# Two-layer attention and gated-MLP kernel: the first two head groups of layer two take turns by key pairs, and head outputs are turned by DMA

## The chip, the cores and the metric

The kernel runs on one core of a Trainium2 chip. Five engines work side by side: PE (TensorE, matmuls into PSUM), ACT (ScalarE), DVE (VectorE), POOL (GpSimd) and SP (SyncE, here only a queue that issues DMA). The metric is the device time of one execution in microseconds.

## The reference

Two layers of multi-query attention, each followed by a gated MLP with a mixing matrix over the sequence. S = 2048 rows, D = 512, 32 heads of 16 with one shared key and value head, F = 1792.

```python
def _A_ref(x, wq, wk, wv, wo):
    q = (x @ wq).reshape(B, S, 32, 16).transpose(0, 2, 1, 3)
    k, v = x @ wk, x @ wv
    p = softmax(einsum('bhqd,bkd->bhqk', q, k) * 16 ** -0.5)
    return einsum('bhqk,bkd->bhqd', p, v).transpose(0, 2, 1, 3).reshape(B, S, 512) @ wo

def _B_ref(x, w_in, w_sp, b_sp, w_out):
    z = gelu(x @ w_in)
    z1, z2 = z[..., :896], layernorm(z[..., 896:])
    g = einsum('ts,bsf->btf', w_sp, z2) + b_sp[None, :, None]
    return (z1 * g) @ w_out

x = x + A(layernorm(x)); x = x + B(layernorm(x))     # layer one
x = x + A(layernorm(x)); x = x + B(layernorm(x))     # layer two, same weights
```

## The kernel before

**Order of the work.** Every operation is handed to a planner (class `Sched`) with an estimated duration, its dependences and a priority. The planner plays the whole kernel through on paper and fixes one instruction order for each engine; on the chip each engine takes its instructions in that order and waits on semaphores. So a small edit can move instructions all over the program.

**Attention.** The rows are cut into query chunks of 512, 512, 512, 256, 128 and 128 (`chunks`). A head group is 4 heads of 512 query columns (or more heads of fewer columns); there are 32 groups a layer, in pairs that share one query set: `kT` holds the keys twice, masked for the even and for the odd half of the heads (`v` = 0 and 1). A unit is one key tile of 128 rows in one group, with four blocks (one for each head row group of 32), each a score matrix of 128 keys by 512 queries. A key pair is two key tiles, and units are worked off in pairs.

Scores (`_qk`, L1710) go into a ring of PSUM banks: `self.ring = [(0, 3), (3, 2)]`, that is banks 0 to 2 and banks 3 and 4 in turn. `FillStream` fills one half, `ExpStream` (L1382) takes the exp of the other half on ACT in one instruction of 3 or 2 blocks (128x1536 or 128x1024) into the SBUF ring `Pa`. While ACT works on one half, PE fills the other. Some blocks go to DVE instead (`DexStream`: L1566, then a chain of five operations L1591 to L1597 on two blocks at a time, into `Pd`), through one of the side banks 5 and 7. `PVStream` (L1458) multiplies the exps with V and accumulates a whole group in bank 6 (`pvb`), four heads side by side. `WarmStream` (L1691) puts in matmuls on zeros where PE would have too little to do.

**End of a group** (`finish_group`): DVE copies bank 6 to `oT` (L826), PE transposes it in four 128x128 pieces into a side bank (L833), DVE takes the reciprocal of the denominators, which come from a column of ones in V (L838), and multiplies (L850) into `on`. When a chunk has all its heads, `project` turns `on` by DMA (L552, for the last two chunks by PE, L886), multiplies by `wo` (L915) and adds to the residual `X` (L919).

**Gated MLP.** `mixer_chunk` normalises, multiplies by `w_in` (L947, L983) and takes the gelu on ACT (L1014, L1018, with table loads). `spatial` multiplies by the mixing matrix in passes over the row tiles that are ready (L1124; its bias starts the first pass with a matmul of 4 rows, L1121), evicted by DVE into `gp` (L1137, L1138). These matmuls run between the attention of the later chunks. The matrix w_sp is transposed by DMA at the start (L591) and kept in a scratch in HBM (L593).

**Closing and the next layer's keys.** The last row tile's part of the mixing can only run when the last chunk is done. `closing` does it in eight steps of 256 rows: matmuls on `z2n` (L1183), a cast to `E` on DVE or ACT (L1194, L1195), add (L1198), multiply with z1 (L1201), matmul with `w_out` (L1216), add to the residual (L1221). After each step, in layer one, `layer_keys` builds one key pair of layer two: layernorm (`ln`: L637 to L652, transposed by DMA, L552, or by PE, L669), keys (L699) and values (L707) and their copies to `kT` (L719 on DVE, L721 on ACT) and `V`. For the value matmul the weight stands four times side by side, padded to 128 columns (`wv_rep`), so that the result has the four copies that P.V reads. During the closing the score ring has only what the key pairs so far allow: group 0 of layer two over the key tiles that exist. `gate` holds DVE's exps of layer two back until the closing has read its buffers.

The units are worked in the order of their list, group after group:

```python
for k in range(self.NT):
    u = Unit()
    u.grp, u.kt, u.index, u.pv = g, k, len(self.units), None
```

Of the kernel before, what the change touches and what calls it, by code (L numbers as in the profile page):

```python
# [13 lines left out]
P = 128  # L14
# [359 lines left out]
LOOK = 7  # L374
# [35 lines left out]
class Group:  # L410

    __slots__ = ("layer", "ci", "v", "t0", "n", "units", "q", "evac", "index")
# [14 lines left out]
class Kern:  # L427
    def __init__(self, nc, A_x, A_wq, A_wk, A_wv, A_wo, B_x, B_w_in, B_w_sp, B_b_sp, B_w_out, out):
# [13 lines left out]
        self.ring = [(0, 3), (3, 2)]  # L442
# [18 lines left out]
        self.wv_rep = sb([P, KD, 128], BF16, "wv_rep")  # L461
        self.wo_r = sb([P, 4, D], BF16, "wo_r")
        self.w_in_r = sb([P, KD, FF], BF16, "w_in_r")
        self.b4 = sb([4, 512], BF16, "b4")
# [22 lines left out]
        self.oT = sb([P, 2, 512], BF16, "oT")  # L487
        self.on = sb([P, 4, D], BF16, "on")
# [42 lines left out]
        sc.lend(1, range(self.ring[1][0], sum(self.ring[1])), None)  # L531
# [26 lines left out]
    def load(self, A_x, A_wq, A_wk, A_wv, A_wo, B_b_sp):  # L558
# [3 lines left out]
        wv_nat = self.z1s[:, 64:128].rearrange("p (kd n) -> p kd n", kd=KD)  # L562
# [7 lines left out]
        lv = self.dma(lambda e: e.dma_start(wv_nat, A_wv.rearrange("(kd p) r -> p kd r", p=P)), (), "ldv", 131072, 1.1,  # L570
# [13 lines left out]
        self.l_b = self.dma(lambda e: e.dma_start(self.b4[:], B_b_sp.rearrange("(k t) -> k t", k=4)), (), "ldb", 4096)  # L584
# [31 lines left out]
        for j in range(4):  # L616
# [5 lines left out]
        m = vm(self.wv_rep[:], 512, 0.12)  # L622
        self.c_wv = rows(self.wv_rep[:].rearrange("p kd (g r) -> p kd g r", r=32)[:, :, :, 0:DH],
                         wv_nat[:, :, None, :].to_broadcast([P, KD, 4, DH]), m, lv, 256, 1.1)
        self.c_wq = [lq[0]] + [lq[1]] * 3
        m = vm(self.V[:], 2048, 0.13)
        self.z1s_free = [self.c_wk, self.c_wv]
# [55 lines left out]
    def layer_keys(self, layer):  # L683
        sc = self.sc
        for p in range(8):
            def build(p=p):
                ts = (2 * p, 2 * p + 1)
                pr = 0.3 if p < 2 else 1.0
                dd = list(self.xnTA_read[p])
                evs = []  # L690
                for tt in ([ts[:1], ts[1:]] if p < 2 else [ts]):
                    evs += self.ln(tt, lambda t: [self.x_op[t]], self.xnTA[:, tt[0]:tt[-1] + 1, :, :], dd, pr, p < 2,
                                   layer == 0)
                self.xnTA_read[p] = []

                def kpe(e, b):
                    ins = None
                    for kd in range(KD):
                        ins = e.matmul(self.b32(b)[:, 0:256], self.wk_rep[:, kd, :], self.xnTA[:, 2 * p:2 * p + 2, kd, :],  # L699
                                       start=(kd == 0), stop=(kd == KD - 1))  # L700
                    return ins

                def vpe(e, b):
                    ins = None
                    for i, t in enumerate(ts):
                        for kd in range(KD):
                            ins = e.matmul(self.b32(b)[:, 256 + 128 * i:384 + 128 * i],  # L707
                                           self.xnTA[:, t, kd, :], self.wv_rep[:, kd, :],
                                           start=(kd == 0), stop=(kd == KD - 1))
                    return ins  # L710

                def kcp(b, v):
                    return self.kT[:, v, p * 256:(p + 1) * 256], self.b32(b)[:, 0:256]

                def vcp(b):
                    return (self.V[:, ts[0]:ts[0] + 2, :].rearrange("p t (c r) -> p t c r", r=32)[:, :, :, 0:DH],
                            self.b32(b)[:, 256:512].rearrange("p (t c r) -> p t c r", t=2, c=4)[:, :, :, 0:DH])
                kd_, vd_ = self.kv_war.get((layer, p), ([], []))
                ks = [dict(fn=lambda e, b, v=v: e.tensor_scalar(*kcp(b, v), self.mask[:, v:v + 1], None, op0=ALU.mult),  # L719
                           dur=d_psum(256), prio=pr - 0.1 + 0.2 * v, deps=kd_ + [self.c_mask[v]],  # L720
                           alts=[("act", lambda e, b, v=v: e.activation(*kcp(b, v), ACTF.Copy, scale=self.mask[:, v:v + 1]),  # L721
                                  d_act(256) + 0.1)]) for v in range(2)]
                vc = dict(fn=lambda e, b: e.tensor_copy(*vcp(b)), dur=d_psum(128), prio=pr, deps=[self.c_v] + vd_,
                          alts=[("act", lambda e, b: e.activation(*vcp(b), ACTF.Copy), d_act(128) + 0.1)])
                if p < 2:
                    _, k = sc.job([(kpe, 4 * d_mm(256))], ks, evs + [self.c_wk], pr)
                    _, (v,) = sc.job([(vpe, 8 * d_mm(128))], [vc], evs + [self.c_wv], 0.9)
                else:
                    _, (k0, v, k1) = sc.job([((lambda e, b: (kpe(e, b), vpe(e, b))[1]), 4 * d_mm(256) + 8 * d_mm(128))],
                                            [ks[0], vc, ks[1]], evs + [self.c_wk, self.c_wv], pr)  # L730
                    k = [k0, k1]
                self.xnTA_ev[(layer, p)] = evs
                for t in ts:
                    self.k_op[(layer, 0, t)], self.k_op[(layer, 1, t)] = k
                    self.v_op[(layer, t)] = v
            if layer == 0:
                build()
            else:
                self.key_builders[p] = build
# [5 lines left out]
    def layer_groups(self, layer):  # L745
        t0 = 0
        for ci, n in enumerate(self.chunks):
            ns = 512 // n
            for s0, v in [(s, v) for s in range(0, 4, ns) for v in range(2)]:
                g = Group()  # L750
                g.layer, g.ci, g.v, g.t0, g.n = layer, ci, v, t0, n
                g.index = len(self.groups)
                if v == 0:
                    q = QSet()
                    q.grp, q.s0, q.ns, q.op, q.left, q.reads = g, s0, ns, None, 8 * self.NT, []
                    q.index = len(self.qsets)
                    q.slot = q.index % NQS
                    self.qsets.append(q)
# [16 lines left out]
            t0 += n  # L775

# [44 lines left out]
    def finish_group(self, g, pv_last):  # L821
# [4 lines left out]
        ev = sc.op("dve", lambda e: e.tensor_copy(self.oT[:, par, :], self.b32(self.pvb)), d_psum(512),  # L826
# [9 lines left out]

        def rc(e, b):
            return e.reciprocal(self.rden[:, par, :, :], self.b16(b)[:, 0:512].rearrange(  # L838
                "p (i j r) -> p i j r", i=4, j=4)[:, :, :, DH])

        def nm(h, e, b):
# [4 lines left out]
            else:  # L846
# [4 lines left out]
                out, self.b16(b)[:, s0 * 128:s1 * 128].rearrange("p (i j r) -> p i j r", j=4, r=32)[:, :, :, 0:DH],  # L851
                self.rden[:, par, s0:s1, :, None].to_broadcast([P, s1 - s0, 4, DH]), ALU.mult)
        hs = range(2 if g.n == 256 else 1)
        pl, ops = sc.job([(pe, 0.3)], [
# [212 lines left out]
    def spatial(self, s0, s1, layer):  # L1067
# [28 lines left out]
        for tc in range(4):  # L1096
# [16 lines left out]
            for f in range(NF):  # L1113
                seq = ([] if acc else [None]) + list(range(s0, s1))

                def pe(e, b, part, tc=tc, f=f, w_=w_, seq=seq):
                    ins = None
                    for s in part:
                        st, sp = (s == seq[0]), (s == seq[-1])
                        if s is None:  # L1120
                            ins = e.matmul(self.b32(b), self.ident[0:4, tc:tc + 1].to_broadcast([4, P]), self.b4[:, :],  # L1121
# [129 lines left out]
class FillStream:  # L1251
# [5 lines left out]
    def __init__(self, k):  # L1257
        self.k = k
        self.u = 0
        self.n = 0  # L1260
        self.exp_of = [None, None]
        self.pending = [False, False]
        self.last = []
# [14 lines left out]
    def peek(self, f):  # L1278
# [4 lines left out]
        self.blocks = self.nxt(k.ring[r][1])  # L1283
        if not self.blocks:
            return None
        deps = [self.exp_of[r]]
        for b in self.blocks:
# [8 lines left out]
        if not k.sc.reclaim(r):  # L1296
            return None
        self.deps = [d for d in deps + k.sc.lent_rel(r) if d is not None]
        return (max([d.vis for d in self.deps], default=0.0), 0.0)

    def commit(self, t):
        k = self.k
        r = self.n % 2
        b0 = k.ring[r][0]
# [32 lines left out]
        self.n += 1  # L1337
        self.last = [o]
        k.exp_s.queue.append((r, blocks, o))


class ExpStream:
# [5 lines left out]
    def __init__(self, k):  # L1348
        self.k = k
        self.queue = []  # L1350
        self.slot = 0
        self.owner = [None] * NPA
# [5 lines left out]
    def peek(self, f):  # L1358
        if not self.queue:
            return None  # L1360
        r, blocks, fo = self.queue[0]
        base = (self.k.ring[r][0] + 5 * self.slot) % NPA
# [11 lines left out]
    def commit(self, t):  # L1374
        k = self.k
        r, blocks, fo = self.queue.pop(0)
        base = self.base
        n = len(blocks)
        b0 = k.ring[r][0]
# [10 lines left out]
        if r == 1:  # L1390
            self.slot = (self.slot + 1) % 3
# [3 lines left out]
        if not nx or nx[0].unit.grp.layer != blocks[0].unit.grp.layer:  # L1395
            k.sc.lend(r, range(b0, b0 + k.ring[r][1]), o)
            if not self.queue:
                k.sc.op("act", lambda e: e.activation(k.tiny[:], k.mhalf[:], ACTF.Gelu_apprx_tanh), 0.1, [o, k.c_mh], -2.0,
                        table="gelu")


class PVStream:
# [5 lines left out]
    def __init__(self, k):  # L1408
        self.k = k
        self.u = 0  # L1410
        self.evac = None

    def peek(self, f):
# [16 lines left out]
        if u.first:  # L1430
            if self.evac is not None:
                if self.evac.start is None:
                    return None
                deps.append(self.evac)
            if not k.sc.reclaim("pv"):
                return None
            deps += k.sc.lent_rel("pv")
# [12 lines left out]
    def commit(self, t):  # L1450
# [3 lines left out]
        def fn(e):  # L1454
            ins = None
            for b in u.blocks:
                j = b.j
                ins = e.matmul(k.b32(k.pvb)[32 * j:32 * j + 32, :], k.V[:, u.kt, 32 * j:32 * j + 32], b.slot,  # L1458
# [7 lines left out]
        if u.last:  # L1466
            k.finish_group(u.grp, o)
            self.evac = u.grp.evac
            if self.u == len(k.units) or k.units[self.u].grp.layer != u.grp.layer:
                self.evac.at_commit = lambda ev: k.sc.lend("pv", [k.pvb], ev)  # L1470
# [179 lines left out]
class WarmStream:  # L1650
# [10 lines left out]
    def peek(self, f):  # L1661
# [9 lines left out]
        if u >= len(k.units) or k.units[u].first:  # L1671
# [3 lines left out]
            else:  # L1675
                ev = k.pv_s.evac
                if ev is None or ev.start is None or u >= len(k.units) or k.units[u].grp.layer != k.units[u - 1].grp.layer:
# [8 lines left out]
    def commit(self, t):  # L1686
        k = self.k
        b = self.bank

        def fn(e):  # L1690
            return e.matmul(k.b32(k.pvb if b is None else b.idx), k.zero[:], k.zero[:, None, :].to_broadcast([P, 4, P]),  # L1691
# [71 lines left out]
```

## Time and profile before

| | us |
|---|---|
| median of 8 runs (lowest 1833.04, highest 1837.45) | 1835.0 |
| the profiled execution | 1834.5 |
| its span, first to last instruction | 1832.4 |
| ACT busy in the span | 1739.7 |
| DVE busy | 1697.8 |
| PE busy | 1599.4 |

PE's busy time holds 327.3 us of matmuls on zeros. The mean granted TensorE clock is 0.993 of full speed. Exps of three blocks show 1600 ns each and exps of two 1176 ns; since one starts before the other has wholly ended, these durations overlap, and the union of all 1430 exps is 1625.2 us. In the lists below, a row names the source line, the engine, the operation, what it writes and reads, and in brackets the idle time before it with what ended it.

### The profile page before, as it was taken

What the parts mean: (1) busy time and instruction counts of PE and PEld (TensorE: products, weight loads), DVE (VectorE), ACT (ScalarE), POOL (GpSimd) and SP (SyncE); (2) the same over time, 40 slices, a digit from 0 to 9 for tenths busy, and PEclk for the clock granted to TensorE, in tenths of its full rate; (3) what the DMA queues carried; (4) which work ended last, traced back from release to release, by engine and by line L of the source; (5) the groups of instructions that cost most, each with busy time, mean ns of one, the idle gap of its engine ahead of it and who ended that gap; (6) DMA issues with size and microseconds to landing.
All of it is one profiled execution on the core that took longest, in us unless ns stands there. A gap on an engine that the chain in (4) does not pass through costs nothing.

```text
span 1832.4 us, 30222 instructions
## 1 busy us (share of the span) xinstructions
PE 1599.4 (87%) x11863; PEld 480.3 (26%) x11947; DVE 1697.8 (93%) x2924; ACT 1739.7 (95%) x1565; POOL 49.1 (3%) x89
## 2 busy tenths in 40 slices
PE   8888888888899998998888888888888999999988
PEld 3222222222222222223432222222222222222234
DVE  8999999999989899887889999999999998998868
ACT  8999999999999999999579999999999999999983
POOL 1000000000000000000100000000000000000000
PEclk9999999989999999999999999999999999999999
DMA  9800010001000111202210000100010000201123
GB/s 264 214 1 1 12 35 1 1 1 21 16 28 24 47 24 36 64 27 56 65 37 1 1 1 13 35 1 1 1 21 12 33 24 24 47 27 41 58 57 111
DMA packets 122964, 68.04 MB, mean 37 GB/s; under 512 B 76996, under 2 KB 119240, under 8 KB 122824
## 3 DMA queue, kind: packets, MB, share of 16 engines
q1 hardware_dynamic: 121240, 65.95, 13.4%
q8 instruction: 95, 1.56, 0.4%
q14 instruction: 45, 0.37, 0.1%
q10 hardware_dynamic: 1584, 0.16, 0.1%
HBM read 30.97 MB, written 17.83 MB: 27 GB/s over the span
## 4 chain that ended last, share of the span: by engine, by line
ACT 42%; PE 22%; DVE 18%; issue 17%; POOL 1%; DMA 0%; ACTq 0%; POOLq 0%
ACT Pa L1382 40%; PE ps_all L1710 6%; PE ps_all L1124 6%; PE ps_all L1458 4%; DVE E L1566 3%; DVE Pd L1597 3%; PE ps_all L1216 2%; PE ps_all L1691 1%; DVE E L1593 1%; DVE E L1591 1%; DVE E L1595 1%; DVE st L637 1%; PE ps_all L915 1%; DVE E L1594 1%; DVE gp L1137 1%
## 5 line engine op out<-in xcount | busy, mean ns | idle before, releaser
L1382 ACT ACTIVATE Pa<-ps_all 128x1536 bf16<-128x1536 f32 (+1 forms) x1430 | 1625.2, 1388 | 14.3 <-PE ps_all L1710 12.4
L1710 PE MATMUL ps_all<-qs,kT 32*128 32x512 bf16 x4096 | 562.7, 386 | 179.7 <-ACT Pa L1382 163.8
L1566 DVE TENSOR_SCALAR E<-ps_all 128x512 f32<-128x512 f32 x522 | 356.0, 685 | 26.1 <-PE ps_all L1710 22.4
L1691 PE MATMUL ps_all<-zero 128*128 128x512 bf16 x1051 | 327.3, 391 | 17.4 <-ACT z1s L1014 3.2
L1710 PEld LDWEIGHTS ps_all<-qs,kT 32*128 32x128 bf16 x4096 | 138.7, 91 | 734.7 <-ACT Pa L1382 685.6
L1458 PE MATMUL ps_all<-Pa,V 128*32 128x512 bf16 x3574 | 324.2, 387 | 0.2 <-ACT Pa L1382 0.2
L1597 DVE SCALAR_TENSOR_TENSOR Pd<-E 128x1024 uint16<-128x1024 f32 (+1 forms) x262 | 318.2, 1214 | 4.1
L1124 PE MATMUL ps_all<-wsT,z2n 128*128 128x512 bf16 x655 | 187.4, 382 | 7.5 <-issue 4.1
L1593 DVE TENSOR_TENSOR E<-E 128x1024 f16<-128x1024 f16 (+1 forms) x262 | 179.2, 684 | 5.2
L1458 PE MATMUL ps_all<-Pd,V 128*32 128x512 bf16 x522 | 183.3, 386 | 0.0
L1595 DVE TENSOR_TENSOR E<-E 128x1024 f16<-128x1024 f16 (+1 forms) x262 | 178.7, 682 | 3.7
L1591 DVE TENSOR_SCALAR E<-E 128x1024 f16<-128x1024 uint16 (+1 forms) x262 | 179.0, 683 | 1.3
L1691 PEld LDWEIGHTS ps_all<-zero 128*128 128x128 bf16 x1051 | 79.8, 98 | 186.5 <-issue 126.8
L1594 DVE TENSOR_SCALAR E<-E 128x1024 f16<-128x1024 f16 (+1 forms) x262 | 109.3, 417 | 1.8
L1137 DVE TENSOR_TENSOR gp<-ps_all,gp 128x512 f16<-128x512 f32 x112 | 75.4, 685 | 26.2 <-PE ps_all L1124 25.9
L1458 PEld LDWEIGHTS ps_all<-Pa,V 128*32 128x32 bf16 x3574 | 64.7, 94 | 121.3 <-issue 117.0
L1124 PEld LDWEIGHTS ps_all<-wsT,z2n 128*128 128x128 bf16 x714 | 54.0, 97 | 98.9 <-issue 59.1
L947 PE MATMUL ps_all<-w_in_r,xnTB 128*128 128x448 bf16 x256 | 63.1, 356 | 1.3 <-DVE E L1566 1.0
L983 PE MATMUL ps_all<-xnTB,w_in_r 128*128 128x512 bf16 (+2 forms) x336 | 61.8, 310 | 0.5 <-DVE z1s L994 0.4
L1216 PE MATMUL ps_all<-E 128*128 128x512 bf16 x215 | 51.6, 380 | 4.7 <-DVE E L1201 3.0
L1195 ACT ACTIVATE E<-ps_all 128x512 f16<-128x512 f32 (+1 forms) x52 | 24.6, 550 | 24.0 <-PE ps_all L1183 24.0
L826 DVE CAST oT<-ps_all 128x512 bf16<-128x512 f32 x64 | 43.8, 685 | 2.9 <-PE ps_all L1458 2.6
(87 smaller groups left out, 949.7 us busy)
## 6 DMA issues: line engine op xcount, KB each, us to landing
wsT_scratch<-gp SPq DMA_DIRECT2D x16, 512.0 KB, 3.8
wsT<-wsT_scratch SPq DMA_DIRECT2D x8, 1024.0 KB, 5.4
z1s<-z_scratch SPq DMA_DIRECT2D x16, 448.0 KB, 3.8
wsT<-wsT_scratch SPq DMA_DIRECT2D x8, 512.0 KB, 3.8
z_scratch<-z1s SPq DMA_DIRECT2D x4, 896.0 KB, 6.4
X<-in_A_x_dram SPq DMA_DIRECT2D x8, 256.0 KB, 5.6
out_dram<-X SPq DMA_DIRECT2D x16, 128.0 KB, 1.9
w_in_r<-in_B_w_in_dram SPq DMA_DIRECT2D x1, 1792.0 KB, 10.0
```

Source lines behind the costliest of these rows:

```text
L1124: ins = e.matmul(self.b32(b), self.z2n[:, s, f * 128:(f + 1) * 128], w_[:, s - s0, :] if s - s0 < na or not spare else wsp[:, s - s0 - na, :],
L1137: return e.tensor_tensor(dst, self.b32(b), dst, ALU.add)
L1382: return e.activation(k.Pa[:, base:base + n, :], k.b32(b0, n).rearrange("p (k q) -> p k q", k=n), ACTF.Exp, scale=SCALE)
L1458: ins = e.matmul(k.b32(k.pvb)[32 * j:32 * j + 32, :], k.V[:, u.kt, 32 * j:32 * j + 32], b.slot, tile_position=(0, 32 * j), start=u.first, ...
L1566: c = k.sc.op("dve", lambda e: e.tensor_scalar(k.ey[:, s, 512 * i:512 * (i + 1)], k.b32(j.bank.idx)[:, 0:512], E_LOG2, E_BIAS, op0=ALU.mul ...
L1591: o2 = sc.op("dve", lambda e: e.tensor_scalar(x, lo, E_X * 2.0 ** -16, E_X * E_A, op0=ALU.mult, op1=ALU.add), d_sb(n, 0.521e-3), self.ops ...
L1593: o3 = sc.op("dve", lambda e: e.tensor_tensor(w, x, x, ALU.mult), d_sb(n, 0.521e-3), [o2, self.wfree], pr)
L1594: o4 = sc.op("dve", lambda e: e.tensor_scalar(w, w, E_C, None, op0=ALU.add), d_sb(n, 0.26e-3), [o3], pr)
L1595: o5 = sc.op("dve", lambda e: e.tensor_tensor(w, w, x, ALU.mult), d_sb(n, 0.521e-3), [o4], pr)
L1597: o7 = sc.op("dve", lambda e: e.scalar_tensor_tensor(po.bitcast(U16), y, E_D, w, op0=ALU.add, op1=ALU.add), d_sb(n, 1.042e-3), [o5] + self ...
L1691: return e.matmul(k.b32(k.pvb if b is None else b.idx), k.zero[:], k.zero[:, None, :].to_broadcast([P, 4, P]), start=b is not None, stop=b ...
L1710: return e.matmul(self.b32(bank), self.kT[32 * j:32 * j + 32, g.v, kt * 128:(kt + 1) * 128], self.qs[32 * j:32 * j + 32, g.q.slot, :], til ...
```

## The change

- Layer two's first two groups (the two halves of one query set) are interleaved in the list of units: two key tiles of the first, the same two of the second, and so on. The second accumulates in bank 0 (`pvb2`).
- The ring has three shapes. While the last key tile of layer two is not yet placed ("ramp"), banks 1 to 3 alone, one fill of three blocks after another, and bank 4 goes to the side jobs. Then, until the second group's copy is placed ("pair"), banks 1, 2 and banks 3, 4 in turn. Otherwise ("full") as before. A change of shape waits until both exps in flight are done.
- Places in `Pa` are handed out one after another, not by fixed slots.
- `wv_r` has the 16 value columns once; the copy from PSUM writes them four times.
- Except in the last chunk, a group's output is turned by a DMA transpose on SP's queue into `oTt`, and the reciprocal and the product read that; the PE transposes and their side bank are not used.
- The bias rows are padded with zeros to 128 rows, the last key pair of layer two is transposed by PE, and DVE's exps look 6 units ahead, not 7 (`LOOK`).

```diff
-LOOK = 7
+LOOK = 6
...
-        self.ring = [(0, 3), (3, 2)]
+        self.rings = {"full": [(0, 3), (3, 2)], "ramp": [(1, 3), (1, 3)], "pair": [(1, 2), (3, 2)]}
+        self.pvb2 = 0
...
-                                   layer == 0)
+                                   layer == 0 or p >= 7)
...
-                            ins = e.matmul(self.b32(b)[:, 256 + 128 * i:384 + 128 * i],
-                                           self.xnTA[:, t, kd, :], self.wv_rep[:, kd, :],
+                            ins = e.matmul(self.b32(b)[:, 256 + DH * i:256 + DH * (i + 1)],
+                                           self.xnTA[:, t, kd, :], self.wv_r[:, kd, :],
...
+        if layer == 1:
+            ga, gb = [g for g in self.groups if g.layer == 1][:2]
+            gb.pvb = self.pvb2
+            self.twin = gb
+            i0 = ga.units[0].index
+            self.units[i0:i0 + 2 * self.NT] = [u for i in range(0, self.NT, 2) for g in (ga, gb) for u in g.units[i:i + 2]]
+            for i, u in enumerate(self.units[i0:i0 + 2 * self.NT]):
+                u.index = i0 + i
...
+        if g.ci < len(self.chunks) - 1:
+            tr = self.transpose(self.oTt[:, par, :].rearrange("p (i r) -> p i r", i=4), self.oT[:, par, :],
+                                [ev, self.rd_read[par]], f"oq{par}", 0.5)
+            self.oT_read[par] = tr
+            m = sc.op("dve", lambda e: rc(e, None), 0.18, [tr], 0.6)
+            for h in hs:
+                m = sc.op("dve", lambda e, h=h: nm(h, e, None), d_psum(256 // len(hs)), [m] + onr, 0.5)
+                self.norms.append(m)
...
+        mode = "full"
+        if self.blocks[0].unit.grp.layer == 1:
+            o = k.k_op.get((1, 0, k.NT - 1))
+            if o is None or o.start is None:
+                mode = "ramp"
+            elif k.twin.evac is None or k.twin.evac.start is None:
+                mode = "pair"
+            else:
+                deps.append(k.twin.evac)
+        if mode != self.mode:
+            if any(self.pending):
+                return None
+            deps += self.exp_of
...
-        self.n += 1
+        self.n += 2 if self.mode == "ramp" else 1
...
-        base = (self.k.ring[r][0] + 5 * self.slot) % NPA
+        base = self.pos if self.pos + len(blocks) <= NPA else 0
```

## The prediction

> **What bounds the kernel now.** I read the page first (busy shares), then the stretches, then ACT's waits, then the timeline of the one stage in which ACT has holes.
>
> ```profile
> span 1832.4 us, 30222 instructions
> PE 1599.4 (87%) x11863; PEld 480.3 (26%) x11947; DVE 1697.8 (93%) x2924; ACT 1739.7 (95%) x1565; POOL 49.1 (3%) x89
> ...
> ACT  8999999999999999999579999999999999999983
> ```
>
> ACT is the bound: 1739.7 of 1832.4 us, so 92.7 us idle in all. Its row of tenths has two holes, in the middle (5, 7) and at the end (8, 3). The stretches size them (columns: PE, PEld, DVE, ACT, POOL busy, TensorE clock, DMA).
>
> ```profile
> 860.00:880.00 20.00, 18.69 (x115) 7.80 (x115) 13.54 (x25) 8.94 (x11) 0.55 (x1) 1.00 0.00 1
> 880.00:900.00 20.00, 16.03 (x118) 9.20 (x118) 18.68 (x55) 10.57 (x23) 2.81 (x5) 1.00 0.24 66
> 900.00:920.00 20.00, 17.72 (x126) 7.68 (x127) 19.02 (x53) 14.36 (x20) 3.05 (x6) 1.00 0.35 89
> 920.00:940.00 20.00, 16.73 (x110) 6.62 (x111) 14.29 (x37) 12.16 (x16) 1.52 (x4) 1.00 0.26 50
> 940.00:960.00 20.00, 16.85 (x126) 5.84 (x124) 17.01 (x33) 15.76 (x17) 1.29 (x3) 0.91 0.13 27
> 980.00:1000.00 20.00, 16.77 (x129) 4.29 (x129) 19.56 (x32) 20.00 (x19) 0.00 (x0) 1.00 0.00 1
> ```
>
> From 860 to 960, where layer one closes and layer two's keys appear, ACT is idle 38.2 us, while DVE is at 18.7 and 19.0 of 20 until 920. The last row is steady attention: ACT full, DVE 98%. Within the hole, ACT's own timeline from the first exp of layer two:
>
> ```profile
> 903.65 6.88 ACT L1382 ACTIVATE Pa<-ps_all 128x1024 bf16<-128x1024 f32 x6 [0.44 <-PE ps_all L1710]
> 915.03 0.47 ACT L721 ACTIVATE kT<-ps_all,mask 128x256 bf16<-128x256 f32 x1 [4.50 <-PE ps_all L707]
> ...
> 935.05 0.60 ACT L1195 ACTIVATE E<-ps_all 128x512 f16<-128x512 f32 x1 [3.56 <-PE ps_all L1183]
> 936.13 1.51 ACT L1195 ACTIVATE E<-ps_all 128x512 f16<-128x512 f32 x3 [0.48 <-PE ps_all L1183]
> 942.55 0.47 ACT L721 ACTIVATE kT<-ps_all,mask 128x256 bf16<-128x256 f32 x1 [4.91 <-PE ps_all L707]
> ```
>
> The waits of 4.50 and 4.91 us end at a key: group 0 has used up every key pair. That is what the change aims at. From 943.74 on ACT is nearly full again. After 903.65 the holes sum to 16.4 us; the 20.8 us before it lie in the tail of the layer, with no score to work on, and the change gives nothing there.
>
> **The change part by part.** Counts come from the instruction orders of the two programs as built, times from the one profiled execution, 1834.5 us (1832.4 of span and 2.1 around it); the median of the runs is 0.5 higher.
>
> *Price of a score block.* Between 79.08 and 240.99 ACT did 143 exps without a gap: 161.9/71.5 = 2.264 us for a pair of 3 and 2 blocks, 0.453 a block. Refills start 0.91 us apart across an exp of 2 blocks and 1.35 across one of 3, so exps of 2 alone cost 0.455 a block.
>
> 1. *Exps.* 714 to 707 of 3 blocks, 716 to 724 of 2; P.V matmuls that read DVE's exp go from 522 to 528. Six blocks fewer on ACT: 6 x 0.453 = -2.7 us. DVE gets three more chains (2 x 0.685 + 0.685 + 0.686 + 0.418 + 0.684 + 1.219 = 5.06 us each, 15.2 in all); its 134.6 us of idle time cover that, at 760 to 860 above all (13 to 17 of 20). If not, P.V of those units is late next, then the exp that wants its buffer.
>
> 2. *Other ACT work.* Layer one loses four key copies of 0.42 net and the V-weight copy of 0.42, and gains a 1024-wide copy (about 1.0), a query copy and a V copy; four 512-wide casts in the closings go to DVE. I take -0.6 us.
>
> 3. *Ramp: two groups on the same keys.* Until the last key tile is planned, scores use one buffer of three banks (1 to 3), with no double buffering. An exp of 3 is 1.60 us to its end, the fill starts 0.07 later, and exp follows fill by 0.43 (903.22 to 903.65): 2.1 us for 3 blocks against 1.35. PE stands in order behind each fill that waits, and the closing's matmuls behind it. I walked the order from the first fill: fourteen fills at 2.1, and where PE puts 9 or 10 matmuls of 0.215 between fills, or ACT casts and key copies, about 2.3: near 31 us to the last closing matmul. DVE was busy about 32.3 of the 38.8 us between 903.2 and the last residual add (942.0); four more casts of 0.6, two of 256 fewer at 0.35, and V copies add 2 us. So 31 from PE and ACT, 34 from DVE; with dependences I take 35.3, that is -3.5 us (ends: -5, and +4 if the two delays add up). At that point 42 blocks have been filled where before had 40: -0.9. Then four single-buffered fills follow where before ran full: 4 x 0.75, less 1.2 for query and key copies that fit the gaps: +1.8. Two changes of ring (ramp to pair, pair to full) each empty it once, fill and latency, 0.6: +1.2. Sum -1.4 us. The pair stage itself is 34 exps of 2: 68 x 0.002 = 0.1, nothing.
>
> 4. *Head outputs turned by DMA.* 240 PE transposes go (256 to 16), 60 DMA transposes come on SP's queue. The nearest row, the same shape:
>
> ```profile
> L552 SPq DMA_TRANSPOSE onT<-on x28: 1191/1267/2222, 222.2 to 1667.5; - x28
> ...
> DMA to landing us min/median/max: 2.4/2.5/4.4
> ```
>
> About 2.5 us after the eviction. In the new order DVE has mostly 3.8 us of work between eviction and reciprocal (about 3.3 with overlaps): hidden. Behind that reciprocal stand DVE's exp chains; at 4.4 us a landing costs 1.1 us of DVE. Ends: 0, and 60 x 1.1 = 66 us of DVE, of which little reaches ACT. I take 0, near the median. On SP six of them stand between the w_sp transposes, so SP waits there for each group; the last w_sp store moves from 78 us to about 47.8 + 5 x 25 = 173, still before its first reader at 261 us. Reciprocal and normalisation now read SBUF. The Trainium skill (VectorE: DVE Perf Modes, Why PSUM operands drop a tier) lets one hope for the two-element mode; 16-bit SBUF products of 256 take 0.285 us here, the PSUM form 0.415, so the rule's best is 64 x 0.13 = 8.3 us of DVE. The second operand stays fp32, so I take 0.415 and no gain. PE relief matters only where PE is at 18.5 of 20 (500 to 660, 1420 to 1560, 1640 to 1680), where ACT is idle 6.8 us: -1.5.
>
> 5. *V unreplicated, bias from 128 rows, last key pair turned on PE, LOOK 6.* 128 V matmuls shrink from 128 to 16 columns; PE does not bound, 0. The V copy keeps its 0.28 us. The bias load waits for a POOL memset, covered by 800 us. LOOK acts through the counts above.
>
> 6. *Ends.* The first fill now stands behind the third key pair: about 1 us later, 0.5 got back by fewer copies: +0.5. After the last P.V, layer one has 39 spatial matmuls left against 31, layer two 45 against 40; at 0.215, partly under the head chain: +0.7 and +0.5. Sum +1.7.
>
> Total: -2.7 - 0.6 - 1.4 - 1.5 + 1.7 = -4.5, so 1830.0 on the profiled run, 1830.5 as a median.
>
> **A rule against the change.** PE loses work and waits more. [...]the clock falls already:
>
> ```profile
> 380.00:400.00 20.00, 16.46 (x117) 4.05 (x116) 17.09 (x27) 18.53 (x18) 0.00 (x0) 0.84 0.00 1
> 400.00:420.00 20.00, 17.47 (x130) 4.17 (x129) 19.12 (x29) 19.19 (x18) 0.00 (x0) 0.90 0.00 1
> ```
>
> ACT lost 2.3 us there. The Trainium skill (TensorE: Matmul & The Clock Gate, HAM oscillation) says a gap of over 3.4 us brings half clock; from these clocks, 10.4 us at half rate, priced by the page at half, 5.2 us of PE. The row decides: 2.3. Sixty more dummy matmuls (1051 to 1111) replace what goes, so I count 0 and keep 2.3 for one more episode, 5.2 at the rule's price.
>
> **The rivals.**
> - *The single buffer stretches the closing (slower).* If PE's wait at each fill is not hidden under DVE, 14 waits of 0.75 add 10.5 us to DVE's chain: 34 + 10.5 = 44.5 against 38.8, +5.7 where I have -3.5. Total +4.7: 1839.7. For it: PE is in order and DVE has no slack at 900 to 920. Against: DVE idles at 920 to 940. It decides from 43 us between first fill and last residual add. Chance 0.23.
> - *Two groups fill the hole.* The ramp holes of 16.4 us all but vanish as the closing runs at 31 us and DVE keeps pace: some 6 us beyond my sum, 1824.5. Against: single buffering. Chance 0.21.
> - *It does not do what it says.* 42 blocks against 40 at the closing's end is hardly more exps; then only items 1 and 6 act: 1834. Chance 0.14.
>
> **How the numbers follow.** My case has 0.42, at 1826 to 1835, about six tenths of it beyond the 0.2% (3.7 us) that a measurement of this kernel can tell. Faster (below 1831.3): 0.25 + 0.21 = 0.46. Within: 0.15 of my case, 0.13 of the last rival, 0.02 of the first: 0.30. Slower (above 1838.7): 0.21 of the first, 0.02 of my case, 0.01 of the last: 0.24. Range 1821 to 1841: from the faster rival less a late clock episode to the slower one plus a little.
>
> **What would show it.** First fill to last residual add: 35 us right, 43 the slower rival, 31 the faster. ACT idle from 860 to 960 (38.2) should fall to about 35. DVE waits at the reciprocal on the DMA beyond 10 us in sum would refute item 4, more than 93 us of ACT idle in all the whole forecast.

## The result, and the profile after

| | before | after |
|---|---|---|
| median, us (32 and 11 runs on one chip) | 1834.19 | 1823.35 |
| lowest and highest | 1831.89 to 1840.25 | 1819.3 to 1833.64 |
| ratio, 95% interval | | 0.9939 [0.9928, 0.9949] |
| the profiled execution; its span | 1834.5; 1832.4 | 1824.4; 1822.6 |

The kernel became faster by 10.8 us, or 0.6%. The sum had said 4.5. First the page of the kernel after: span, busy times, and ACT's row of tenths.

```profile
span 1822.6 us, 29937 instructions
PE 1587.7 (87%) x11690; PEld 467.4 (26%) x11775; DVE 1709.5 (94%) x2947; ACT 1735.8 (95%) x1563; POOL 50.8 (3%) x90
...
ACT  7999999999999999999589999999999999999983
```

ACT is still the bound. The 9.8 us by which the span shrank are 3.9 us less work on ACT (1739.7 to 1735.8) and 5.9 us less idle time (92.7 to 86.8). The middle hole, tenths 5 and 7 before, is 5 and 8. The same stretches as before (columns: PE, PEld, DVE, ACT, POOL busy, TensorE clock, DMA):

```profile
860.00:880.00 20.00, 17.69 (x123) 8.41 (x123) 16.30 (x31) 9.13 (x13) 1.10 (x2) 1.00 0.00 1
880.00:900.00 20.00, 16.47 (x116) 9.26 (x119) 19.58 (x59) 10.39 (x24) 2.26 (x4) 1.00 0.30 82
900.00:920.00 20.00, 18.06 (x126) 7.29 (x125) 19.61 (x53) 15.50 (x19) 2.82 (x6) 1.00 0.41 96
920.00:940.00 20.00, 16.84 (x136) 7.50 (x134) 17.00 (x46) 14.74 (x18) 2.98 (x6) 0.91 0.21 41
940.00:960.00 20.00, 16.77 (x140) 4.99 (x140) 19.73 (x33) 19.19 (x22) 0.00 (x0) 1.00 0.00 1
980.00:1000.00 20.00, 16.80 (x131) 4.17 (x131) 19.69 (x32) 20.00 (x19) 0.00 (x0) 1.00 0.00 1
```

The two rows before 900 have hardly moved: there is still no score to work on. From 900 to 960 ACT is busy 49.43 us where it was 42.28. All of ACT's idle time, by stretch:

| stretch, us | idle before | idle after | change |
|---|---|---|---|
| 0 to 20 (first scores) | 8.3 | 9.8 | +1.5 |
| 20 to 840 (layer one) | 5.9 | 2.7 | -3.2 |
| 840 to 860 | 0.0 | 1.9 | +1.9 |
| 860 to 960 (closing, ramp) | 38.2 | 31.05 | -7.2 |
| 960 to 980 (change of ring) | 0.0 | 0.5 | +0.5 |
| 980 to 1700 | 5.4 | 5.2 | -0.2 |
| 1700 to the end | 34.85 | 35.5 | +0.7 |

So the ramp is where most came from. Layer one, which the interleave does not touch, gave 3.2 us up to 840 and took 1.9 of them back. ACT's timeline through the ramp, from the first exp of layer two on:

```profile
901.35 1.45 ACT L1428 ACTIVATE Pa<-ps_all 128x1536 bf16<-128x1536 f32 x1 [1.10 <-PE ps_all L1761]
903.72 1.45 ACT L1428 ACTIVATE Pa<-ps_all 128x1536 bf16<-128x1536 f32 x1 [0.92 <-PE ps_all L1761]
...
935.96 1.45 ACT L1428 ACTIVATE Pa<-ps_all 128x1536 bf16<-128x1536 f32 x1 [1.35 <-PE ps_all L1761]
...
942.35 1.45 ACT L1428 ACTIVATE Pa<-ps_all 128x1536 bf16<-128x1536 f32 x1 [0.50 <-PE ps_all L1761]
943.70 0.47 ACT L722 ACTIVATE kT<-ps_all,mask 128x256 bf16<-128x256 f32 x1
944.28 2.85 ACT L1428 ACTIVATE Pa<-ps_all 128x1024 bf16<-128x1024 f32 x3
947.32 28.61 ACT L1428 ACTIVATE Pa<-ps_all 128x1024 bf16<-128x1024 f32 x31 [0.18 <-PE ps_all L1761]
976.42 60.31 ACT L1428 ACTIVATE Pa<-ps_all 128x1536 bf16<-128x1536 f32 x53 [0.49 <-PE ps_all L1761]
```

Eighteen exps of three blocks (54 blocks) come 2 to 3.7 us apart, each after a wait for the single buffer's refill or beside other ACT work. The pair stage follows at 944.28, and the full ring at 976.42. Of ACT's waits for a key, one of 0.8 us is left. In the list of ACT's waits over the whole run (total, times, longest) the second pair is of before, the first of after:

```profile
ACT Pa L1428 <- PE ps_all L1761: 17.4, 26, 1.7
...
ACT kT L722 <- PE ps_all L708: 0.8, 1, 0.8
```

```profile
ACT Pa L1382 <- PE ps_all L1710: 12.4, 34, 1.0
ACT kT L721 <- PE ps_all L707: 11.1, 6, 4.9
```

The wait for keys fell by 10.3 us, and the wait for refilled scores rose by 5.0, about half as much. In the 120 us after the first exp of layer two, whose rows stand further down, it rose from 2.6 to 9.1: that is the price of the single buffer.

The head outputs (the product of 256 columns and the reciprocal, before and then after; behind them the DMA transposes on the tile `oTt` and their landing):

```profile
L850 DVE TENSOR_TENSOR on<-ps_all,rden 128x256 bf16<-128x256 bf16 x56 | 23.2, 415 | 0.1
L838 DVE RECIPROCAL rden<-ps_all 128x16 f32<-128x16 bf16 x64 | 16.1, 252 | 7.2 <-PE ps_all L833 6.9
```

```profile
L863 DVE TENSOR_TENSOR on<-oTt,rden 128x256 bf16<-128x256 bf16 x52 | 21.6, 415 | 0.1
L851 DVE RECIPROCAL rden<-oTt 128x16 f32<-128x16 bf16 x60 | 14.9, 248 | 3.2 <-DMA oTt<-oT 3.2
```

```profile
L555 SPq DMA_TRANSPOSE oTt<-oT x60: 1189/1192/1541, 49.2 to 1709.0; - x60
...
DMA to landing us min/median/max: 2.4/2.4/4.5
```

DVE stood still for a landing 3.2 us in all, where it had stood 7.2 us for PE's transposes, and the reciprocal takes 248 ns from SBUF where it took 252 from PSUM.

### The profile page after: what moved, and what is told of

It is laid out like the page before. It is cut to its first block, busy times and chain, and to the rows that moved or that the text cites. A ratio compares the mean times of both kernels' runs of the same rounds, so it can differ in the third digit from the quotient of the medians.

```text
span 1822.6 us, 29937 instructions
## 1 busy us (share of the span) xinstructions
PE 1587.7 (87%) x11690; PEld 467.4 (26%) x11775; DVE 1709.5 (94%) x2947; ACT 1735.8 (95%) x1563; POOL 50.8 (3%) x90
## 4 chain that ended last, share of the span: by engine, by line
ACT 43%; DVE 20%; issue 18%; PE 18%; DMA 1%; POOL 0%; ACTq 0%; POOLq 0%
ACT Pa L1428 41%; PE ps_all L1761 5%; PE ps_all L1152 4%; PE ps_all L1507 3%; DVE E L1615 3%; DVE Pd L1646 2%; PE ps_all L1244 2%; DVE E L1642 2%; DVE E L1644 1%; DVE E L1640 1%; DVE st L638 1%; PE ps_all L1742 1%; DVE gp L1165 1%; DVE E L1643 1%; ACT z1s L1042 1%
## 5 line engine op out<-in xcount | busy, mean ns | idle before, releaser
L1428 ACT ACTIVATE Pa<-ps_all 128x1024 bf16<-128x1024 f32 (+1 forms) x1431 | 1623.0, 1380 | 20.0 <-PE ps_all L1761 17.4
L1742 PE MATMUL ps_all<-zero 128*128 128x512 bf16 x1111 | 343.4, 390 | 16.3 <-DVE mv L1068 4.6
L1646 DVE SCALAR_TENSOR_TENSOR Pd<-E 128x1024 uint16<-128x1024 f32 x265 | 321.9, 1215 | 4.4
L1152 PE MATMUL ps_all<-wsT,z2n 128*128 128x512 bf16 x671 | 192.7, 382 | 7.6 <-issue 2.9
L1642 DVE TENSOR_TENSOR E<-E 128x1024 f16<-128x1024 f16 x265 | 181.5, 685 | 4.5
L1644 DVE TENSOR_TENSOR E<-E 128x1024 f16<-128x1024 f16 x265 | 181.2, 684 | 3.7
L1640 DVE TENSOR_SCALAR E<-E 128x1024 f16<-128x1024 uint16 x265 | 180.7, 682 | 1.2
L1643 DVE TENSOR_SCALAR E<-E 128x1024 f16<-128x1024 f16 x265 | 110.9, 418 | 2.2
L642 POOL TENSOR_SCALAR ve<-mv 128x2 f32<-128x2 f32 (+1 forms) x28 | 9.7, 347 | 1384.8 <-DVE mv L640 1384.7
```

The costliest lines, as they stand in the source:

```text
L1152: ins = e.matmul(self.b32(b), self.z2n[:, s, f * 128:(f + 1) * 128], w_[:, s - s0, :] if s - s0 < na or not spare else wsp[:, s - s0 - na, :],
L1428: return e.activation(k.Pa[:, base:base + n, :], k.b32(b0, n).rearrange("p (k q) -> p k q", k=n), ACTF.Exp, scale=SCALE)
L1640: o2 = sc.op("dve", lambda e: e.tensor_scalar(x, lo, E_X * 2.0 ** -16, E_X * E_A, op0=ALU.mult, op1=ALU.add), d_sb(n, 0.521e-3), self.ops ...
L1642: o3 = sc.op("dve", lambda e: e.tensor_tensor(w, x, x, ALU.mult), d_sb(n, 0.521e-3), [o2, self.wfree], pr)
L1643: o4 = sc.op("dve", lambda e: e.tensor_scalar(w, w, E_C, None, op0=ALU.add), d_sb(n, 0.26e-3), [o3], pr)
L1644: o5 = sc.op("dve", lambda e: e.tensor_tensor(w, w, x, ALU.mult), d_sb(n, 0.521e-3), [o4], pr)
```

## The experiments

Two theories stood at the start. *Ramp:* the interleave lets ACT do work during the closing that it did after it, and this is the gain. *Plan:* the change moves the order of the whole program, and most of the gain is a luckier order, in layer one and late in layer two. The first four runs take the two large parts away, one and both, and give the ramp a double buffer; the next four move LOOK, which changes the plan and, for each step down, hands DVE 3 to 8 more of the 4096 score blocks. In each, 5 rounds were timed against the kernel before on the same chip (1833.32 us for the first four, 1832.54 for the others). The expectations come first; all runs stand in one table behind them.

**Without the interleave, DMA turn kept.** The units stay in group order and the ring is full throughout.

```diff
-        if layer == 1:
+        if False:
             ga, gb = [g for g in self.groups if g.layer == 1][:2]
...
-        if self.blocks[0].unit.grp.layer == 1:
+        if False:
             o = k.k_op.get((1, 0, k.NT - 1))
```

> The changed kernel with its units in the old order (group after group) and the ring always full; DMA-turned outputs, unreplicated V and LOOK 6 stay. Theory A (two groups on the same keys end ACT's wait for keys): about 1829 us, of the 10.8 us gained some 5 to 6 are lost again, and ACT's idle time from 860 to 960 us is back near 38. Theory B (PE and a side bank freed by the DMA transposes bring the gain): 1824, no loss that can be told.

**Interleave kept, head outputs turned by PE.**

```diff
-        if g.ci < len(self.chunks) - 1:
+        if False:
             tr = self.transpose(self.oTt[:, par, :].rearrange("p (i r) -> p i r", i=4), self.oT[:, par, :],
```

> The changed kernel with head outputs turned by PE as before; interleaving, unreplicated V and LOOK 6 stay. Theory A: 1824 to 1825, at most 1.5 us lost, since PE does not bound. Theory B: 1829 to 1832, most of the gain lost, with ACT idle in the stages of spatial matmuls.

**Neither.** Both edits at once; V unreplicated, the bias of 128 rows, the last key pair on PE, the packed places in `Pa` and LOOK 6 remain.

> The changed kernel with both undone; only unreplicated V, padded bias, the last key pair on PE and LOOK 6 stay. Both theories: 1830 to 1834, close to the kernel before. If it is below 1827 the small edits or the planner's reshuffling brought most of the gain, which neither theory says.

**A double buffer in the ramp.**

```diff
-"ramp": [(1, 3), (1, 3)]
+"ramp": [(1, 2), (3, 2)]
...
-        self.n += 2 if self.mode == "ramp" else 1
+        self.n += 1
```

> The changed kernel with the ramp on two halves of two banks (1, 2 and 3, 4), not one of three: scores are double-buffered from the first fill, and the closing has side banks 5 and 7 alone. If the single buffer is what leaves ACT the holes of 0.5 to 1.7 us between the ramp's exps, ACT's idle time from 900 to 945 falls from about 10 to under 5 and the time to about 1819. If the closing's pace (DVE's chain, side banks) sets the end of the ramp, it is drawn out by the exps and banks taken from it: 1823 to 1828.

**LOOK alone.** The kernel before with LOOK 6; the kernel with neither part and LOOK 7; the changed kernel with LOOK 7 and with LOOK 5.

```diff
-LOOK = 7
+LOOK = 6
```

> The kernel before with LOOK 6 alone. Theory C (the horizon of DVE's exps is what the small edits gain by): 1824 to 1826, as good as the kernel with the small edits alone (1823.6). Theory D (the gain is in the padded bias, the 16-column V, the last key pair on PE, or the packed exp buffer): within 2 us of before, 1831 to 1835. In between: both.

> The small edits alone as in the run with neither interleaving nor DMA-turned outputs, but LOOK 7 as before. Theory C: back to 1831 to 1834. Theory D: stays at 1823 to 1826.

> The changed kernel with LOOK 7. Theory C: about 1830, since LOOK carries the gain that the small edits showed. Theory D: 1822 to 1826. A distance of some us either way also measures what a reshuffled plan is worth by itself.

> The changed kernel with LOOK 5: 536 score blocks on DVE in place of 528, ACT 8 fewer, 8 x 0.453 = 3.6 us. Theory C: up to 1820, as the horizon shortens further. Theory D: no trend with LOOK, within 3 us of 1823.

**What was measured.** "Layer one" is the time from its first exp to its last; "closing" runs from the first exp of layer two to the end of the last residual add of layer one's closing; "blocks" are the score blocks that ACT and DVE had begun in the 120 us after the first exp of layer two, when every version is in the steady state; "opening" runs from that first exp to the start of the copy that takes the fourth group of layer two out of PSUM. Times are of one profile each. The ratio is the one on record; it differs from the quotient of the two medians by up to 0.0012.

| kernel | median, us | ratio to before [95%] | layer one | closing | blocks | opening |
|---|---|---|---|---|---|---|
| before | 1834.19 | 1 | 850.6 | 38.3 | 243 | 128.1 |
| before, LOOK 6 | 1825.82 | 0.9968 [0.9956, 0.9980] | 849.3 | 39.1 | 245 | 127.9 |
| neither, LOOK 7 | 1830.45 | 0.9987 [0.9978, 0.9995] | 849.0 | 39.9 | 243 | 128.5 |
| neither | 1823.58 | 0.9953 [0.9941, 0.9966] | 844.4 | 41.0 | 243 | 127.9 |
| no interleave | 1830.41 | 0.9989 [0.9980, 0.9998] | 846.3 | 41.7 | 234 | 131.7 |
| **after** | 1823.35 | 0.9939 [0.9928, 0.9949] | 847.9 | 35.0 | 254 | 124.4 |
| interleave, PE turn | 1820.86 | 0.9944 [0.9931, 0.9956] | 844.4 | 33.9 | 255 | 125.3 |
| after, LOOK 7 | 1819.66 | 0.9934 [0.9922, 0.9946] | 848.1 | 32.8 | 259 | 123.3 |
| after, LOOK 5 | 1820.63 | 0.9941 [0.9927, 0.9956] | 845.0 | 32.7 | 258 | 123.0 |
| after, ramp doubled | 1823.92 | 0.9957 [0.9945, 0.9970] | 849.4 | 51.8 | 260 | 122.3 |

**How the expectations came out.** Without the interleave, theory A's signs came: 1830.41 us and ACT idle 38.5 us from 860 to 960. With the PE turn, theory B's loss did not come. With neither, 1823.58 us is what both theories had excluded. With the double buffer, ACT's idle time from 900 to 945 fell from 10.4 to 3.5 us as said, but the time did not fall to 1819; the other branch, a closing that is drawn out, had 1823 to 1828. LOOK alone did what theory C said for the kernel before (1825.82) and nearly so for the one with neither part (1830.45), but not in the changed kernel, where LOOK 7 gave 1819.66 and not 1830.

**The ramp theory holds for its stage.** Five versions without the interleave need 127.9 to 131.7 us for the opening, five with it 122.3 to 125.3; the two sets do not touch, and the means differ by 5.2 us. The version with the ramp doubled is among the short ones (122.3), so it is the second group that shortens the opening, and not the single buffer. The blocks say the same without any mark of a group's end. The rows of the exps by shape, in the 120 us after the first exp of layer two (count behind the x): before, without the interleave, after.

```profile
L1382 ACT ACTIVATE Pa<-ps_all 128x1536 bf16<-128x1536 f32 x43 | 69.8, 1624 | 1.8 <-PE ps_all L1710 1.8
L1382 ACT ACTIVATE Pa<-ps_all 128x1024 bf16<-128x1024 f32 x43 | 51.3, 1192 | 0.8 <-PE ps_all L1710 0.8
```

```profile
L1428 ACT ACTIVATE Pa<-ps_all 128x1536 bf16<-128x1536 f32 x42 | 67.4, 1605 | 1.7 <-PE ps_all L1761 1.7
L1428 ACT ACTIVATE Pa<-ps_all 128x1024 bf16<-128x1024 f32 x41 | 48.4, 1179 | 2.0 <-PE ps_all L1761 1.8
```

```profile
L1428 ACT ACTIVATE Pa<-ps_all 128x1536 bf16<-128x1536 f32 x38 | 56.9, 1498 | 8.8 <-PE ps_all L1761 8.8
L1428 ACT ACTIVATE Pa<-ps_all 128x1024 bf16<-128x1024 f32 x54 | 53.9, 1108 | 0.3 <-PE ps_all L1761 0.2
```

That is 215, 208 and 222 blocks on ACT, although ACT waited longest in the last. DVE's chains of two blocks add 14, 13 and 16 of them (windows of the chain's last operation in before and in after; the count is in brackets):

```profile
903.45:1023.65 120.20, 17.05 (x14) 0.99 0.12 26
```

```profile
901.15:1021.35 120.20, 19.21 (x16) 0.99 0.13 27
```

In all 243, 234 and 254. The steady state does about 26.5 blocks in 10 us (the 128 blocks of two groups in the 48.4 us between before's second and fourth copy, shown in the next section), so the 11 blocks between before and after are about 4 us.

**The single buffer, with the bank that it frees, does not stretch the closing; it shortens it.** The residual adds of the closing, from the answer on that line between 900 and 960 (durations; first and last start): before, after, and with the ramp doubled.

```profile
L1221 DVE TENSOR_TENSOR X<-ps_all,X x11: 657/683/693, 900.1 to 941.3; 128x512 bf16<-128x512 f32 x11
```

```profile
L1249 DVE TENSOR_TENSOR X<-ps_all,X x10: 656/678/692, 902.5 to 935.7; 128x512 bf16<-128x512 f32 x10
```

```profile
L1249 DVE TENSOR_TENSOR X<-ps_all,X x11: 657/691/693, 899.6 to 953.8; 128x512 bf16<-128x512 f32 x11
```

With two buffers, 88 blocks are filled before the closing's last matmul (42 in after), and the closing ends 51.8 us after the first exp, not 35.0. Yet the lead of 40 exps of two blocks after 43 us against 18 of three has shrunk to 260 against 254 blocks at 120 us, and the time is no better: 0.9957 against 0.9939, with intervals that overlap. What the scores win during the closing, the closing loses, and the other way round. A run with the one buffer but without the interleave was not made, so how much of the shorter closing is due to the buffer and the lent bank, and how much to the second group, stays open.

**The plan theory holds in part, and over half of what LOOK alone moves goes with the clock.** LOOK moves the kernel before by 0.32% and the kernel with neither part by 0.34%, each about 6 us, both down for 6; in the changed kernel LOOK 5, 6 and 7 give 0.9941, 0.9939 and 0.9934, all within one another's intervals. So the parts do not add. At LOOK 7 both parts together are worth 0.0053 (9.7 us); at LOOK 6 the same two are worth 0.0014 (2.6 us, intervals overlapping). The opening is shorter in both cases: 128.5 to 123.3, and 127.9 to 124.4. At LOOK 6 the difference is lost in layer one (844.4 to 847.9 in the profiles, 1.9 of it by a fall of the clock).

The record has the mean granted clock of every run, and within one kernel the time goes with it: the changed kernel took 1819.3 us at 0.997 and 1833.64 at 0.986, about 1.3 us for each 0.001. LOOK shows in this clock. The kernel before ran at 0.998 to 1.000 with LOOK 6, and at 0.991 to 0.998 with LOOK 7 on the same chip. Where both ran at 0.998, they took 1825.77 to 1828.34 (three runs) and 1828.81 (one run), so, as far as one run can tell, over half of the 6 us goes with the clock. The gain of the interleave does not. These are the runs without and with it at one and the same clock:

| pair | clock | without | with | opening shorter by |
|---|---|---|---|---|
| no interleave; after | 0.997 | 1829.36 to 1830.41 (4 runs) | 1819.3, 1819.45 | 7.3 |
| neither; after, both LOOK 7 | 0.997 | 1828.35 to 1829.67 (4 runs) | 1818.97, 1819.66 | 5.3 |
| neither; interleave, PE turn | 0.998 | 1823.58 to 1824.41 (3 runs) | 1820.86 | 2.6 |

The shorter opening makes up more than half of each difference (some 11, 10 and 3 us). Where the rest comes from, and why the first two pairs gain so much more than the third, stays open; the runs at one clock are few, the two kernels of the first pair were not timed together, and the second pair also differs in the DMA turn.

**The DMA turn costs time without the interleave, and none that can be told with it.** Without, it goes with 0.0036 more (0.9953 to 0.9989), 3.8 us of it in the opening (127.9 to 131.7); with it 0.0005 less (0.9944 to 0.9939, intervals overlapping). Why is open. Its two single versions at LOOK 7 were not run.

None of these versions is shown to beat the changed kernel: the lowest ratio, 0.9934 with LOOK 7, lies inside its interval.

## Why the prediction was right, and where its sum was short

*The direction and the mechanism* were right, and two tests came out as written: first fill to last residual add 35.4 us (35.3 said; the first fill is 0.4 us ahead of the exp at 901.35), and ACT idle of 86.8 us, under 93. The size was not: 10.8 us came where 4.5 were said, and part of it (layer one, below) came with the granted clock and is luck.

*Items 1 and 2 (less work on ACT)* said -2.7 and -0.6; ACT's busy time fell by 3.9. Right, within 0.6.

*Item 3 (ramp)* said -1.4 and is the term that was mis-sized. Measured from the first exp, so that the earlier start of layer two (903.65 to 901.35) does not count, the stage up to the full ring gained about 5. Its -3.5 for the closing was right. The term "four single-buffered fills follow where before ran full: +1.8" was wrong in its premise: before did not run full there. Between its last residual add at 942.0 and about 951.5, before finished 14 blocks, 40 to 54, in 9.5 us where a full ACT needs 14 x 0.453 = 6.3, with the clock at 1.00 all that time. The row 940 to 960 that the prediction itself showed has ACT at 15.76 of 20. After did its 12 blocks, 42 to 54, in 7.5 us (936.3 to 943.8), hardly slower than before's rate of 8.1 for 12. The term is about -0.6. The ring changes, priced +1.2, cost 0.2 and 0.5 (the waits at 947.32 and 976.42), since other work and the pair's own fills overlap most of the drain. Block by block: the 54th is done at 943.8 against about 951.5, and the 122nd, at the end of the pair stage, at 975.9 against about 983.1. Of those 7.2 us, 2.3 came in with the start. The test "38.2 to about 35" for the idle time from 860 to 960 missed by the same error: 31.05.

This lead lasts. The copies of the second and fourth group of layer two out of PSUM, before and then after (DVE's timeline):

```profile
983.40 0.69 DVE L826 CAST oT<-ps_all 128x512 bf16<-128x512 f32 x1
...
1031.80 0.68 DVE L826 CAST oT<-ps_all 128x512 bf16<-128x512 f32 x1
```

```profile
974.81 0.68 DVE L836 CAST oT<-ps_all 128x512 bf16<-128x512 f32 x1
...
1025.75 0.68 DVE L836 CAST oT<-ps_all 128x512 bf16<-128x512 f32 x1
```

The fourth copy comes 6.1 us earlier, the end of the span 9.8.

*Item 4 (DMA turn)* said 0 on DVE: 3.2 us of waits in sum, far from the 10 that would have refuted it, and 4.0 less than before's 7.2 for PE's transposes, which the sum did not have; 2.4 us of median landing against the 2.5 used. No gain from SBUF was right too: the product of 256 takes 415 ns in both kernels. The two-element mode that the forecast hoped for from the Trainium skill (VectorE: DVE Perf Modes, Why PSUM operands drop a tier) did not show with an fp32 operand. "PE relief: -1.5" is not shown: from 980 to 1700 ACT's idle time fell by 0.2, and the versions without the DMA turn are as fast.

*Item 5* said that LOOK acts through the counts alone. It is the second miss: LOOK alone moved the kernel before by about 6 us, of which the counts explain 1.4 (3571 blocks on ACT against 3574, at 0.453). Much of the rest goes with the clock, by the runs at one clock above. The rows of before that stand under "A rule against the change" look like this with LOOK 6:

```profile
380.00:400.00 20.00, 16.21 (x133) 4.17 (x132) 19.46 (x32) 20.00 (x19) 0.00 (x0) 1.00 0.00 1
400.00:420.00 20.00, 16.64 (x136) 4.42 (x129) 19.40 (x30) 20.00 (x19) 0.00 (x0) 1.00 0.00 1
```

PE is no busier, but the clock stays up and the 2.3 us of idle time are gone. Little of LOOK's gain lies here, though: layer one is 1.3 us shorter in the profile, and the stretch from the fourth copy to the last exp 8.4 (745.6 to 737.2). The changed kernel has no fall there either, which is most of its -3.2 in layer one. That this part of the gain comes with a new order, and not from the interleave, is what the versions with LOOK alone suggest; which of the moved instructions keeps the clock up was not found.

*Item 6 (ends)* said +1.7. The first exp is 1.0 us later (14.6 to 15.6), as said; the gap between the layers (last exp to first) went from 38.4 to 37.9 and the tail after the last exp from 55.0 to 54.4, where +0.7 and +0.5 were said. The longer tails of spatial matmuls are covered.

*The rule against the change* was priced at 2.3 us for one more fall of the clock. What came is not one more: the mean clock is 0.993 before and 0.994 after, and the falls have moved, from 380 to 420, 940, 1100 and 1420 to 840, 920, 1400 and 1640. The one at 840 to 860 cost 1.9, but it is not the change's own (see the last section). Half clock, as the Trainium skill has it (TensorE: Matmul & The Clock Gate, HAM oscillation), is what the trace shows: 0.50 from 394 to 403 in before. A gap of over 3.4 us is not: the longest wait of PE is 2.1 us in before and 1.7 in after, and rows with PE at 16.03 of 20 keep the clock at 1.00. What brings a fall stays open.

*The rivals.* "The single buffer stretches the closing" is refuted: 35.4, not 43. "Two groups fill the hole" named nearly the time (1824.5), but its closing of 31 us did not happen; ACT still has some 9 us of gaps in the ramp, where before had 16.4. "It does not do what it says" fell with the blocks: 54 against 40 at 943.8.

## What to carry to other kernels

Where the work of one stage is limited by inputs that come slowly, take a second consumer of the same inputs into it, and count the finished units at a fixed time after the start, not the busy shares: that showed a gain of 5 us that the total hid in some versions. Before you charge a new stage for running at less than full rate, read what the old kernel did in those microseconds. And where a planner orders the whole program, run the change under two or three settings of a knob that hardly matters, and compare runs at the same granted clock: here the knob alone moved the time by 6 us, over half of what the change did, and much of that went with the clock.

## What the runs showed of the hardware

The granted clock falls at different places in executions of one and the same order. The changed kernel, the version without the interleave and the one with the ramp doubled share the whole instruction order of layer one; the stretches (after, without the interleave and ramp doubled at 840; after and ramp doubled at 740; without the interleave at 500) differ all the same:

```profile
840.00:860.00 20.00, 19.51 (x116) 5.33 (x116) 7.82 (x13) 18.11 (x16) 0.00 (x0) 0.84 0.37 101
```

```profile
840.00:860.00 20.00, 19.09 (x131) 5.67 (x135) 9.53 (x15) 20.00 (x19) 0.32 (x1) 1.00 0.40 110
```

```profile
840.00:860.00 20.00, 18.39 (x111) 4.98 (x112) 7.65 (x13) 18.20 (x16) 0.93 (x2) 0.83 0.43 119
```

```profile
740.00:760.00 20.00, 18.56 (x140) 5.11 (x142) 19.93 (x35) 20.00 (x18) 0.00 (x0) 1.00 0.19 47
```

```profile
740.00:760.00 20.00, 18.72 (x135) 5.13 (x139) 18.60 (x33) 18.49 (x17) 0.00 (x0) 0.96 0.19 47
```

```profile
500.00:520.00 20.00, 14.54 (x64) 3.86 (x62) 18.62 (x40) 19.70 (x10) 2.64 (x2) 0.91 0.28 93
```

Each of these falls costs ACT between 0.3 and 1.9 us. Their layer one lasted 847.9, 846.3 and 849.4 us; less the idle time of the falls (1.9; 0.3 at 500; 1.5 at 740 and 1.8 at 840) these are 846.0, 846.0 and 846.1. So a difference of 2 us between two single profiles of this kernel is not yet one of the programs, and the column of layer one in the table above is to be read with that.
